# Step 7's transposes of queries and keys from TensorE to the DMA queue, with its attention one dense piece later

## The chip, the cores and the metric

The kernel runs on one core of one Trainium2 chip. The metric is the time of one execution on the device in microseconds (us), the median of three runs; lower is better. A separate execution was taken by the hardware profiler, and every line of a profile below comes from that one.

The core has TensorE (PE in the profile, its weight loads PEld), VectorE (DVE), ScalarE (ACT), GpSimd (POOL), SyncE (SP) and 16 DMA engines. Engines work through their own instruction streams in order and wait for each other by semaphores. SP issues nearly all DMAs of this kernel.

## What is computed

A decayed linear attention over 4 batches, 8 heads, 768 positions and 64 channels, and behind it a GELU layer without biases:

```python
for b in range(nb):                      # blocks of 64 positions
    intra = einsum('bhic,bhjc->bhij', qb, kb) * Dmask     # lam**(i-j), i >= j
    out[:, :, sl] = einsum('bhij,bhjd->bhid', intra, vb) \
                  + einsum('bhid,bhde->bhie', qb * lam_pow, kv_state)
    kv_state = lam_block * kv_state + einsum('bhsd,bhse->bhde', kb * rev_pow, vb)
x = out.transpose(0, 2, 1, 3).reshape(3072, 512)
h = x @ w_in                             # 512 -> 2048
g = gelu_tanh(h)
y = g @ w_out                            # 2048 -> 512
```

All inputs and the output are float32 in DRAM; the kernel casts to float16 for TensorE.

## The kernel before, in words

The attention is cut into 24 **steps**. A step is one batch, 256 positions and four of the eight heads; steps 2n and 2n+1 are the two halves of the heads of block n. For each step:

- `load_step` (L59, the DMA at L70) loads q, k and v of the step, 256 KB each, on SP's queue. Each of the three has four buffers (pool `ld`), so a load of step s waits until the cast of step s-4 has read its buffer.
- `cast_q` (L282, VectorE) scales q by the decay and casts it, `cast_k` (L295, mostly ScalarE) casts k, `scale_v` (L266, GpSimd) scales and casts v. `prep(s)` is all of them, with the transposing DMA between and further loads after it.
- q and k are needed with channels on partitions. Up to step 7, `stage_t` (L309) does this with eight TensorE transposes (L321) into PSUM and a copy back by ScalarE (L328, steps 5, 6) or VectorE (L330, steps 4, 7). From step `FIRST_DMA_T` = 8 on (L39), `transpose_dma` (L297) issues one DMA transpose on SP (L303) right behind the casts, and `stage_t` does nothing.
- `scores` (L344, matmuls L350) multiplies k by q for the step, `causal` masks the result (L360, VectorE), `products` (L365) multiplies by v, and `update` (L535) carries the state on (`t` on VectorE, `u` on GpSimd).

`R(n, s)` puts scores of step n, products of step n and the second products of step s = n-1 into the streams, then the masks and half of the state's update; `U(n)` is the other half. In later stages `burst` takes two steps at a time.

The GELU layer runs in seven groups of 256 or 512 tokens. `queue_group` cuts the group's matmuls into **dense pieces** (a list called `filler`), and `fill(n)` puts the next n pieces into TensorE's stream. A piece of the first product (`mm1`, L609, matmuls L613) in the groups of 256 tokens is eight matmuls into one PSUM bank, then a GELU on ScalarE (L617). A second product is eight matmuls (L692) of gT or of a sum of parts of gT that VectorE forms (L662): the product is done by a scheme with seven partial products in place of eight.

The order is written out by hand at the end of the kernel (L1043 on), and `pin` keeps it. The scheduler does not move anything. Around the change it reads: `prep(7)`, two pieces, `R(6, 5)`, `U(6)`, a piece, `prep(8)`, a piece, `stage_t(7)`, two pieces, `R(7, 6)` with `prep_qk(9)` between its scores and products, `store_pair(0)` (two output stores on SP), `U(7)`, `scale_v(9)`, two pieces, and then the loop over steps 8 to 12.

SP's queue, in order, around the change: loads of step 8; loads of step 9 (from `prep_v(6)`, L256); q and k of step 10 (from `prep_v(7)`); the DMA transpose of step 8; loads of step 11; the DMA transpose of step 9; v of step 10; the two output stores; the DMA transpose of step 10.

All PSUM tiles share one pool of eight banks (tag M), taken in turn.

Of the kernel before, what the change touches and what calls it, by code (L numbers as in the profile page):

```python
# [15 lines left out]
def kernel(  # L16
# [19 lines left out]
    NF = DFF // P  # L36
    NC = DM // P
    NSTEP = B * NSB * 2
    FIRST_DMA_T = 8  # L39
    PSUM = bass.MemoryType.PSUM  # L40

    const = ctx.enter_context(tc.tile_pool(name="const", bufs=1))
# [17 lines left out]
    def load_step(s, names="qkv"):  # L60
        b, r = divmod(s, 2 * NSB)
        sb, half = divmod(r, 2)
        ts = ld32.setdefault(s, [])
        for nm, src in (("q", q), ("k", k), ("v", v)):
            if nm not in names:
                continue
            t = ld.tile([P, HH, 2, D], FP32, tag=nm + "32", name=f"{nm}32_{s}")
            rows = src[b, half * HH : (half + 1) * HH, sb * SB : (sb + 1) * SB, :]
            queue = nc.scalar if (nm, s) == ("v", 0) else nc.sync
            pin(queue.dma_start(out=t[:].rearrange("p h j d -> p h (j d)"),  # L70
                                in_=rows.rearrange("h (p j) d -> p h (j d)", j=2)))
            ts.append(t)
# [49 lines left out]
    def sum_wout(j, m, eng):  # L122

        a, op, b = W_SUMS[m]
        r = slice(4 * j, 4 * j + 4)

        def rows(t):
            if t in w_slot:
                return w_sum16[:, w_slot[t], r, :]
            f, e = t  # L130
            return w_out16[:, f * HF + r.start : f * HF + r.stop, e * HE : e * HE + HE]

        pin(eng.tensor_tensor(rows(m), rows(a), rows(b), op))
# [36 lines left out]
    def load_ahead(s):  # L170
        if s < NSTEP:
            load_step(s)
# [72 lines left out]
    def prep(s):  # L245
        prep_qk(s)
        prep_v(s)
# [7 lines left out]

    def prep_v(s):  # L256
        scale_v(s)
        if s >= 6:
            if s + 3 == FIRST_DMA_T + 2:
                load_step(s + 3, "qk")  # L260
            else:
                load_ahead(s + 3)

    def scale_v(s):
        tv = a16p.tile([P, 2, HH, D], FP16, tag="v16", name=f"v16_{s}")
        pin(nc.gpsimd.tensor_tensor(wide(tv[:]), ld32[s][2][:], decay(dv, s), ALU.mult))  # L266
        a16[s] = a16[s] + (tv,)

    def prep_qk(s):
        cast_qk(s)  # L270
        transpose_dma(s)

    def cast_qk(s):
        cast_q(s)
        cast_k(s)
# [23 lines left out]
    def transpose_dma(s):  # L299
        tqk = whole_qk.pop(s)  # L300
        if s >= FIRST_DMA_T:
            o = qkp.tile([P, 2, 2, 2, P], FP16, tag="qkT", name=f"qkT_{s}")
            pin(nc.sync.dma_start_transpose(out=o[:].rearrange("p a j h t -> p (a j h) t"),  # L303
                                            in_=tqk[:].rearrange("p a j h d -> p (a j h d)")))
            qkT[s] = o
            if s == FIRST_DMA_T + 1:
                load_step(s + 1, "v")

    def stage_t(s):  # L309
        if s >= FIRST_DMA_T:  # L310
            return
        tq, tk = a16[s][:2]
        if s < 4:
            Tps = [ps_M.tile([P, 2, 2, P], FP16, tag="M", name=f"Tps{i}") for i in range(2)]
        else:
            Tps = ps_M.tile([P, 2, 2, 2, P], FP16, tag="M", name="Tps")
        for i, t in enumerate((tq, tk)):
            to = Tps[i] if s < 4 else Tps[:, i]
            for hp in range(2):
                for j in range(2):  # L320
                    pin(nc.tensor.transpose(to[:, j, hp, :], t[:, j, 2 * hp : 2 * hp + 2, :],  # L321
                                            ident[:]))
        o = qkp.tile([P, 2, 2, 2, P], FP16, tag="qkT", name=f"qkT_{s}")
        if s < 4:
            pin(nc.scalar.activation(out=o[:, 0], in_=Tps[0][:], func=AF.Copy))
            pin(nc.vector.tensor_copy(out=o[:, 1], in_=Tps[1][:]))
        elif s in (5, 6, 8):
            pin(nc.scalar.activation(out=o[:], in_=Tps[:], func=AF.Copy))  # L328
        else:
            pin(nc.vector.tensor_copy(out=o[:], in_=Tps[:]))  # L330
        qkT[s] = o
# [12 lines left out]
    def scores(n):  # L344
        o = qkT[n]
        Sps = [ps_M.tile([P, 2, 2, P], FP32, tag="M", name=f"S{hl}") for hl in range(2)]
        for hp in range(2):
            for jk in range(2):
                for hl, c in TILES:
                    pin(nc.tensor.matmul(  # L350
                        Sps[hl][half64(c), hp, jk, :], o[half64(hl), 1, jk, hp, half64(c)],
                        o[half64(hl), 0, :, hp, half64(c)], start=True, stop=True,
                        skip_group_check=True))
        Ss[n] = Sps

    def causal(n):

        t = ptp.tile([P, 2, 2, 2, P], FP16, tag="PT", name=f"PT_{n}")
        for hl, Sps in enumerate(Ss.pop(n)):
            pin(nc.vector.tensor_tensor(  # L360
                t[:, hl].rearrange("p b c d -> p b (c d)"), Sps[:].rearrange("p b c d -> p b (c d)"),
                mask[:].unsqueeze(1).to_broadcast([P, 2, 2 * P]), ALU.mult))
        PTs[n] = t
# [171 lines left out]
    def update(s, c, parts="tu"):  # L535


        sbg, half = divmod(s, 2)
        sb = sbg % NSB
        if c == 1 and sb == NSB - 1:  # L540
            Kps.pop(s)
            return
        if "t" in parts:
            K = (Kps[s] if c == 0 else Kps.pop(s))[c].rearrange("p (hp d) -> p hp d", hp=2)
            t = ucp.tile([P, 2, D], FP32, tag=f"t{half}", name=f"t_{s}_{c}")
            if sb == 0 and c == 0:
                pin(nc.vector.tensor_copy(out=t[:], in_=K))
            else:
                for hp in range(2):
                    pin(nc.vector.scalar_tensor_tensor(  # L550
                        t[:, hp, :], state[half][:, hp, :],
                        lamu[:, 2 * half + hp : 2 * half + hp + 1], K[:, hp, :],
                        ALU.mult, ALU.add))
            state[half] = t
        if "u" in parts:
            if (s if c == 0 else s + 2) in NARROW:
                u = ubp.tile([P, 2, 2, D], FP16, tag=f"u{half}", name=f"u_{s}_{c}")[:, 0]
                pin(nc.gpsimd.tensor_tensor(  # L558
                    u, state[half][:],
                    lamu[:, 2 * half : 2 * half + 2].unsqueeze(2).to_broadcast([P, 2, D]),  # L560
                    ALU.mult))
                us[(s, c)] = u
                return
            u = ubp.tile([P, 2, 2, D], FP16, tag=f"u{half}", name=f"u_{s}_{c}")
            pin(nc.gpsimd.tensor_tensor(  # L565
                u[:], state[half][:].unsqueeze(2).to_broadcast([P, 2, 2, D]),
                lumask[:, 2 * half : 2 * half + 2, :].unsqueeze(3).to_broadcast([P, 2, 2, D]),
                ALU.mult))
            us[(s, c)] = u
# [21 lines left out]
    def store_pair(pair):  # L591
        rows = out[2 * pair * P : 2 * pair * P + 2 * P, :].rearrange("(i p) d -> p i d", p=P)
        for i in range(2):
            pin(nc.sync.dma_start(out=rows[:, i], in_=o_pairs[pair][:, i]))
# [368 lines left out]
    def fill(n):  # L963
        for _ in range(min(n, len(filler))):
            filler.pop(0)()

    def R(n, s, ahead=None, keep=False):

        def first():
            if n is not None:  # L970
                scores(n)
            if ahead:
                ahead()

        if s in NARROW:
            products(n, s, between=first)
        else:
            first()
            products(n, s)
        if n is not None:  # L980
            causal(n)
        if s is not None and s % 2 == 1:
            g, i = group_of[s // 2]
            if i == len(groups[g]) - 1 and g > 0:
                queue_group(g)
        if n is not None and not keep:
            update(n, 0)

    def U(n):
        update(n, 1)  # L990


    idle(2, 512)
    prep(0)
    stage_t(0)
    chunk_decay()
    idle(1)
    prep(1)
    R(0, None)
    idle(0, 384)  # L1000
    stage_t(1)
    idle(3)
    U(0)
# [3 lines left out]
    causal(1)  # L1007
    idle(2)
    stage_t(2)
    prep_qk(3)  # L1010
    update(1, 0)
# [64 lines left out]
    fill(1)  # L1076
    prep(8)
    fill(1)
    stage_t(7)
    sum_wout(1, 4, DVE)  # L1080
    fill(2)
    R(7, 6, lambda: prep_qk(9))
    store_pair(0)
    U(7)
    scale_v(9)
    fill(2)

    FILL = {8: (2, 0, 0, 0), 9: (1, 2, 1, 2), 10: (0, 1, 1, 3), 11: (0, 1, 1, 3), 12: (0, 2, 1, 3)}
    for n, (a, b, c, d) in FILL.items():
# [135 lines left out]
```

## Time and profile before

| | |
|---|---|
| median of three runs | 198.35 us (198.2 to 198.77) |
| the profiled execution's own time | 198.35 us |
| its span, first to last instruction | 196.5 us |
| granted TensorE clock | 1.000 |
| TensorE transposes (L321) | 64, eight for each of steps 0 to 7 |
| DMA transposes (L303) | 16, steps 8 to 23 |

How to read the profile: the page shows the busy time of each engine, and the span in 40 slices of 4.9 us with the busy share of each engine in tenths. The timeline gives start, duration, engine, line, operation, tiles (written <- read) and count, with the idle time before it and what ended that in brackets; "SPq" rows are DMAs being issued by SP, and their time is that of the issue, not of the transfer. The DMA view adds the time from the issue to the landing of the last byte.

### The profile page before, as it was taken

What the parts mean: (1) busy time and instruction counts of PE and PEld (TensorE: products, weight loads), DVE (VectorE), ACT (ScalarE), POOL (GpSimd) and SP (SyncE); (2) the same over time, 40 slices, a digit from 0 to 9 for tenths busy, and PEclk for the clock granted to TensorE, in tenths of its full rate; (3) what the DMA queues carried; (4) which work ended last, traced back from release to release, by engine and by line L of the source; (5) the groups of instructions that cost most, each with busy time, mean ns of one, the idle gap of its engine ahead of it and who ended that gap; (6) DMA issues with size and microseconds to landing.
All of it is one profiled execution on the core that took longest, in us unless ns stands there. A gap on an engine that the chain in (4) does not pass through costs nothing.

```text
span 196.5 us, 5993 instructions
## 1 busy us (share of the span) xinstructions
PE 190.4 (97%) x2467; PEld 139.2 (71%) x2469; DVE 145.7 (74%) x291; ACT 125.7 (64%) x248; POOL 68.5 (35%) x85
## 2 busy tenths in 40 slices
PE   8979999999999999999999999999999999999993
PEld 2556544456888888754688754578888888888882
DVE  4897722888989879959989826999557996487620
ACT  3663878358774796676856379844877856679221
POOL 6594213457444832528523416064002030002000
PEclk9999999999999999999999999999999999999999
DMA  5999999999999999989999999900520300020205
GB/s 166 291 323 385 384 385 386 302 293 276 267 218 239 262 199 220 239 137 220 361 240 273 251 333 164 227 6 0 36 95 32 110 5 0 3 107 31 79 15 198
DMA packets 62810, 38.13 MB, mean 194 GB/s; under 512 B 18624, under 2 KB 55744, under 8 KB 62784
## 3 DMA queue, kind: packets, MB, share of 16 engines
q1 hardware_dynamic: 62240, 37.50, 76.1%
q8 instruction: 19, 0.31, 0.6%
q10 hardware_dynamic: 544, 0.26, 0.5%
q14 instruction: 7, 0.06, 0.1%
HBM read 27.26 MB, written 6.29 MB: 171 GB/s over the span
## 4 chain that ended last, share of the span: by engine, by line
PE 89%; SPq 4%; DMA 4%; ACT 0%; issue 0%
PE Hps L613 25%; PE MX L692 18%; PE MY L692 9%; PE HX L796 7%; PE O2ps L628 7%; PE MW L692 4%; DMA wi<-in_moe_w_in_dram 4%; SPq L70 4%; PE HY L796 4%; PE S L350 3%; PE Hps L895 3%; PE HW L796 2%; PE O L460 1%; PE OK L400 1%; PE Tps L321 1%; PE OK L422 1%
## 5 line engine op out<-in xcount | busy, mean ns | idle before, releaser
L613 PE MATMUL Hps<-xT,w_in 128*128 128x512 f16 (+1 forms) x288 | 50.5, 332 | 0.0
L613 PEld LDWEIGHTS <-w_in 128*128 128x128 f16 x288 | 27.8, 98 | 19.4
L617 ACT ACTIVATE gT<-Hps 128x512 f16<-128x512 f32 x56 | 32.6, 597 | 9.2 <-PE Hps L613 8.7
L360 DVE TENSOR_TENSOR PT<-S,mask 128x512 f16<-128x512 f32 x48 | 30.3, 681 | 8.8 <-PE S L350 8.8
L266 POOL TENSOR_TENSOR v<-v,dv 128x512 f16<-128x512 f32 x24 | 27.4, 1147 | 19.9 <-DMA v<-in_v_dram 11.5
L692 PEld LDWEIGHTS <-gs 128*128 128x128 f16 x320 | 31.1, 98 | 3.7
L692 PEld LDWEIGHTS <-gT 128*128 128x128 f16 x240 | 23.1, 98 | 3.5 <-ACT gT L617 0.2
L565 POOL TENSOR_TENSOR u<-t,lumask 128x256 f16<-128x256 f32 x21 | 15.6, 758 | 22.1 <-DVE t L550 13.0
L692 PE MATMUL MX<-w_sum,gs 128*128 128x256 f16 x160 | 21.4, 273 | 0.0
L295 ACT ACTIVATE qk<-k 128x512 f16<-128x512 f32 x23 | 14.4, 625 | 7.3 <-DMA k<-in_k_dram 7.1
L282 DVE TENSOR_TENSOR qk<-q,dq 128x512 f16<-128x512 f32 x23 | 17.9, 780 | 1.1 <-DMA q<-in_q_dram 1.1
L749 POOL TENSOR_TENSOR o<-u,q 128x512 f32<-128x512 f32 (+1 forms) x5 | 5.6, 1120 | 37.3 <-issue 34.8
L662 DVE TENSOR_TENSOR gs<-gT 128x1024 f16<-128x1024 f16 (+1 forms) x24 | 16.4, 689 | 3.0 <-ACT gT L617 3.0
L558 POOL TENSOR_TENSOR u<-t,lamu 128x128 f16<-128x128 f32 x19 | 11.2, 597 | 18.7 <-DVE t L550 8.9
L628 PE MATMUL O2ps<-w_out,gT 128*128 128x512 f16 x64 | 14.6, 379 | 0.0
L796 PEld LDWEIGHTS <-ws 128*128 128x128 f16 x128 | 12.4, 98 | 1.7 <-DVE xs L775 0.3
L529 ACT ACTIVATE xT<-OK 128x256 f16<-128x256 f32 x22 | 8.7, 454 | 6.4 <-PE OK L413 3.1
L714 ACT ACTIVATE u<-MX 128x256 f32<-128x256 f32 x18 | 6.9, 383 | 7.4 <-PE MX L692 7.4
L628 PEld LDWEIGHTS <-gT 128*128 128x128 f16 x64 | 6.1, 98 | 6.6
L692 PE MATMUL MY<-w_out,gs 128*128 128x256 f16 x80 | 10.7, 273 | 0.0
L810 DVE COPY u<-HX 128x512 f32<-128x512 f32 x8 | 5.5, 689 | 6.8 <-ACT gT L814 4.4
L350 PEld LDWEIGHTS <-qkT 64*64 64x64 f16 x384 | 6.3, 106 | 5.8 <-issue 2.8
(105 smaller groups left out, 328.5 us busy)
## 6 DMA issues: line engine op xcount, KB each, us to landing
q<-in_q_dram SPq DMA_DIRECT2D x24, 256.0 KB, 4.9
k<-in_k_dram SPq DMA_DIRECT2D x24, 256.0 KB, 5.1
v<-in_v_dram SPq DMA_DIRECT2D x23, 256.0 KB, 5.3
out_dram<-o SPq DMA_DIRECT2D x23, 256.0 KB, 4.5
wo<-in_moe_w_out_dram SPq DMA_DIRECT2D x4, 1024.0 KB, 9.5
wi<-in_moe_w_in_dram SPq DMA_DIRECT2D x4, 512.0 KB, 8.1
wi<-in_moe_w_in_dram SPq DMA_DIRECT2D x2, 1024.0 KB, 13.8
v<-in_v_dram ACTq DMA_DIRECT2D x1, 256.0 KB, 4.3
```

What stands on the lines that cost most here:

```text
L266: pin(nc.gpsimd.tensor_tensor(wide(tv[:]), ld32[s][2][:], decay(dv, s), ALU.mult))
L282: pin(q_eng.tensor_tensor(wide(tq), q32[:], decay(dq, s), ALU.mult))
L295: pin(nc.scalar.activation(out=wide(tk), in_=k32[:], func=AF.Copy))
L350: pin(nc.tensor.matmul(Sps[hl][half64(c), hp, jk, :], o[half64(hl), 1, jk, hp, half64(c)], o[half64(hl), 0, :, hp, half64(c)], start=True, ...
L360: pin(nc.vector.tensor_tensor(t[:, hl].rearrange("p b c d -> p b (c d)"), Sps[:].rearrange("p b c d -> p b (c d)"), mask[:].unsqueeze(1).t ...
L565: pin(nc.gpsimd.tensor_tensor(u[:], state[half][:].unsqueeze(2).to_broadcast([P, 2, 2, D]), lumask[:, 2 * half : 2 * half + 2, :].unsqueez ...
L613: pin(nc.tensor.matmul(by_block(Hps[:, i, :]), w_in16[:, c, f * P : (f + 1) * P], x(c), start=(c == 0), stop=(c == NC - 1)))
L617: pin(nc.scalar.activation(out=dst, in_=Hps[:], func=AF.Gelu_apprx_tanh))
L628: pin(nc.tensor.matmul(O2[tau][0][:], gT[:, f % HF, f // HF, tau * P : (tau + 1) * P], w_out16[:, f, :], start=(n == 0), stop=(n == NF - 1)))
L662: pin(nc.vector.tensor_tensor(g_rows(m, i), g_rows(a, i), g_rows(b, i), op))
L692: pin(nc.tensor.matmul(dst, lhsT, rhs, start=(opens and i == 0), stop=(closes and i == HF - 1), skip_group_check=True))
L796: pin(nc.tensor.matmul(dst[:, i, :], w_in_block(a, slice(c, c + 1), slice(f * P, f * P + P))[:, 0], x_block(b, slice(c, c + 1))[:, 0], sta ...
```

## The change

`FIRST_DMA_T` goes from 8 to 7: step 7 is transposed by the DMA, issued in `prep_qk(7)`, and its eight TensorE transposes and the copy of their result go. The loads of step 9, which `prep_v(6)` issued before, are issued right behind this transpose. One dense piece moves from behind `R(7, 6)` to ahead of it. `prep_qk(9)`, which stood between scores and products of `R(7, 6)`, is put behind `R(7, 6)`, `U(7)` and one piece. That v of step 10 is loaded behind the transpose of step 9 stays as it is.

```diff
-    FIRST_DMA_T = 8
+    FIRST_DMA_T = 7
...
     def prep_v(s):
         scale_v(s)
-        if s >= 6:
-            if s + 3 == FIRST_DMA_T + 2:
-                load_step(s + 3, "qk")
-            else:
-                load_ahead(s + 3)
+        if s == 7:
+            load_step(s + 3, "qk")
+        elif s > 7:
+            load_ahead(s + 3)
...
             qkT[s] = o
-            if s == FIRST_DMA_T + 1:
+            if s == 7:
+                load_step(s + 2)
+            elif s == 9:
                 load_step(s + 1, "v")
...
-        elif s in (5, 6, 8):
+        elif s in (5, 6):
...
     prep(8)
     fill(1)
-    stage_t(7)
     sum_wout(1, 4, DVE)
-    fill(2)
-    R(7, 6, lambda: prep_qk(9))
+    fill(3)
+    R(7, 6)
+    U(7)
+    fill(1)
+    prep_qk(9)
     store_pair(0)
-    U(7)
     scale_v(9)
-    fill(2)
```

## The prediction

> **What bounds the kernel now.** I read the page first: engine shares, then the slices.
>
> ```profile
> span 196.5 us, 5993 instructions
> ...
> PE 190.4 (97%) x2467; PEld 139.2 (71%) x2469; DVE 145.7 (74%) x291; ACT 125.7 (64%) x248; POOL 68.5 (35%) x85
> ...
> PE   8979999999999999999999999999999999999993
> ...
> DMA  5999999999999999989999999900520300020205
> ```
>
> The reader is to see two full rows. TensorE is at 9 from the fourth slice (15 us) to the last, at granted clock 1.00, so every microsecond taken from its queue there is a microsecond of the span, unless it then waits for something. The DMA row is full too, up to slice 26 (127 us): transfers up to there stand in one line, and one more in that line makes all behind it late. The list of waits agrees: the waits of TensorE's weight loads after 30 us sum to about 5 us, mostly "issue" gaps of 0.1 to 0.4 us where the shape of the matmuls changes, and none is for a DMA. So I looked next at the place of the change, in TensorE's timeline:
>
> ```profile
> 50.15 0.61 PE L321 MATMUL Tps<-ident,qk 128*128 128x128 f16 x8
> 50.59 1.91 PE L613 MATMUL Hps<-xT,w_in 128*128 128x256 f16 x16
> 52.43 0.42 PE L350 MATMUL S<-qkT 64*64 64x128 f16 x16
> ...
> 58.69 0.42 PE L350 MATMUL S<-qkT 64*64 64x128 f16 x16
> ```
>
> The transposes of step 7 (L321) hold TensorE from 50.15 to 50.59, scores of step 7 start at 52.43, of step 8 at 58.69. Then SP's queue, and ScalarE's cast of k of step 7:
>
> ```profile
> 45.02 0.78 SPq L70 DMA_DIRECT2D v<-in_v_dram  x1
> 45.89 0.71 SPq L70 DMA_DIRECT2D q<-in_q_dram  x1
> ...
> 49.22 0.58 SPq L70 DMA_DIRECT2D k<-in_k_dram  x1
> 50.81 1.76 SPq L303 DMA_TRANSPOSE qkT<-qk  x1
> 52.63 0.56 SPq L70 DMA_DIRECT2D q<-in_q_dram  x1
> ```
>
> ```profile
> 47.09 0.63 ACT L295 ACTIVATE qk<-k 128x512 f16<-128x512 f32 x1 [0.15 <-ACT qkT L328]
> ```
>
> Here v of step 8 is issued, then q of step 9, up to k of step 10; then the DMA transpose of step 8. Landings are the issue plus the "us to landing" that the DMA view gives for that one issue: v of step 8 at 45.02 + 5.0 = 50.0, k of step 10 at 49.22 + 5.1 = 54.3, transpose of step 8 at 50.81 + 4.5 = 55.3, q of step 11 at 52.63 + 4.8 = 57.5.
>
> **The change, part by part.**
>
> 1. *Eight transposes leave TensorE.* They cost it the distance to the next matmul, 50.59 - 50.15 = 0.44 us (not 8 times the row's mean of 219 ns, as they overlap). This is on the path: **-0.44 us**, and it is the most that the change can give.
> The Trainium skill, "TensorE: Matmul & The Clock Gate", Part 4 (PE-mode transpose), gives about 275 ns for one 128x128 transpose inside a kernel; by that the gain would be 8 x 0.275 = 2.2 us (an estimate from the page). The row of this case, 55 ns each in sequence, decides.
>
> 2. *VectorE's copy of them* (L330, 50.79, 0.69 us) goes as well. VectorE is not on the path there: worth 0.
>
> 3. *One dense piece (8 matmuls, 0.87 us) moves ahead of the attention.* It is moved, not added: 0. Scores of step 7 now start at 52.43 - 0.44 + 0.87 minus the wait for the old copy, about 52.8 (eight matmuls at 49.27, then 24 from 50.15 at 0.109 us). Five pieces instead of six stay between them and scores of step 8, which are wanted at 58.69 - 0.44 = 58.25.
>
> 4. *A new wait: scores of step 7 on a DMA.* The transpose can be issued when k of step 7 is cast, 47.09 + 0.63 = 47.7, plus 0.2 (step 8: cast ends 50.6, issue 50.8): 47.9. Its price from both sides:
>
> ```profile
> L303 SPq DMA_TRANSPOSE qkT<-qk x16: 1232/1622/3359, 50.8 to 139.2; - x16
> ...
> DMA to landing us min/median/max: 4.1/4.6/6.0
> ```
>
> so it lands between 52.0 and 53.9; needed at 52.8. The 4.1 belong to issues with at most 3 us of loads ahead of them (at 80.00 and 83.39), 5.6 and more to those with over 4 us ahead. At 47.9 only q, k, v of step 8 are in flight, the last landing at 50.0, that is 2.1 us: I take 4.1 to 4.5, **landing 52.0 to 52.4, no wait**, with 0.4 to 0.8 us to spare. At 6.0 it is a wait of 1.1 us, and all of TensorE stands behind it.
>
> 5. *The queue behind it.* The transpose passes q, k, v of step 9 and q, k of step 10 on SP, which issue at about 49.3 instead of 45.9. Before, these five came from 50.0 to 54.3, 0.86 each. Now they start from 52.0-52.4; the first load behind a transpose landed 0.9 us after it behind step 10's, 2.2 behind step 8's. So k of step 10 lands at 52.2 + 0.9 to 2.2 + 4 x 0.86 = 56.5 to 57.8, **late by 2.2 to 3.5 us**; I take 2.2 to 2.5, as the new transpose stands in a queue that has nearly drained. Transpose of step 8 follows 1.0 behind as before: 57.5 to 58.8, wanted at 58.25. I take 57.7: no wait; upper end 0.5.
> The page "DMA: Bandwidth & Descriptors" of the Trainium skill, section "Latency and other measured facts", gives DMA transposes an effective 261 GB/s. For these 256 KB that is 1.0 us (an estimate), with which nothing below would be late and the full 0.44 us would come; the 2.15 us between the landings at 55.3 and 57.5 say otherwise.
>
> What else has cover for 2.2 to 2.5 us? Landing against scores, before: step 9 60.1/64.3, step 10 64.7/68.7, step 11 68.8/74.1, step 12 73.9/80.0, step 14 84.1/87.3. The smallest spare is 3.2 us, 2.8 when TensorE is 0.44 earlier: enough. The exception is step 16:
>
> ```profile
> 87.82 1.57 SPq L303 DMA_TRANSPOSE qkT<-qk  x1
> ```
>
> ```profile
> 93.55 0.64 PE L350 MATMUL S<-qkT 64*64 64x128 f16 x32
> ```
>
> It landed at 87.82 + 5.8 = 93.6; these 32 matmuls are steps 15 and 16, so step 16 starts 0.2 after 93.55, at about 93.8. **Only 0.15 us to spare.** What the queue is late there, TensorE waits. But the queue stands still before it:
>
> ```profile
> 83.50:84.50 1.00, 1.00 (x6) 0.47 (x5) 1.00 (x2) 0.60 (x1) 1.00 (x2) 1.00 0.01 2
> ```
>
> (last columns: DMA share 0.01, 2 GB/s). The transpose of step 15 waits there for its own casts. And the loads issued at 71.66 and 78.32 landed in 3.2 and 3.5 us, against 5.0 in the full queue, so the line is short there too; I take half a microsecond from each. So 2.2 to 2.5 late shrinks by about 2, to 0.2 to 0.5 at step 16; the bounds are -0.44 (it comes earlier, with the casts that follow TensorE) and +1.5 (only the 1 us of standstill is won back). With 0.15 us of spare, being 0.2 to 0.5 late would leave TensorE no gain at all here; but a queue that stands still waits for casts, and these come 0.44 earlier. I take the middle between keeping all and losing two thirds: **0.15 us** of the 0.44.
>
> 6. *q and k casts of step 9 move behind the attention.* VectorE's (L282, 52.40, 0.68 us) now runs after masks and state of step 7, at about 55.3; its load lands at 53.1 to 54.4, so it does not wait, but the sums of gT behind it (L662) and the masks of step 8 (59.25) move by about 0.5. The tightest reader is the product that starts at 62.13 and wants, 0.44 later, the sum that ended at 61.73: 0.8 us to spare, minus 0.5, minus 0.44 of gain. Between 0 and 0.4 us; I take **0.1**. ScalarE's k cast has gT evictions behind it, 0.6 us of every 0.87, which catch up: 0.
>
> Sum: -0.44 + 0.15 + 0.1 = **-0.2 us**. The profiled execution took 198.35 us, the same as the median of the runs shown, so 198.35 - 0.2 = **198.15 us**.
>
> **The rivals.**
>
> - *The whole queue stays late up to step 16* (slower). For it: DMA share about 1 in nearly every slice before 83.5, and 0.15 us of spare. Against: the 1 us standstill. It decides from 0.15 us late at step 16, where the time goes above that of before; from part 5's bounds, 0.7 to 1.5 late gives +0.55 to +1.35: 198.9 to 199.7, middle 199.3.
> - *The new transpose is late itself*, 5.6 to 6.0 us: a wait of 0.7 to 1.1 at scores of step 7, and the load queue as much later, which gives 0 to 0.7 again at step 8: net +0.3 to +1.4, 199.1.
> - *The change gives nothing*: what TensorE wins is taken by VectorE's chain (part 6, upper end) and step 16: 198.35 to 198.7.
> - *More than 0.44*: only if the transposes cost TensorE more than their distance, or small gaps close: 197.4 to 197.7.
>
> **How the numbers follow.** 0.3% of this kernel is 0.6 us, about what a measurement of it can tell from no change. The forecast (197.9 to 198.5) gets 0.46, step 16 late 0.28, step 7 late 0.12, nothing gained 0.10, more than 0.44 0.04. Faster by over 0.3% means below 197.75: the last case and a bit of the first, 0.05. Slower means above 198.95: three quarters of the second and of the third case plus a tail of the fourth, 0.33. Within: 0.62. The range goes from 197.8 to 199.6: it leaves out the last case, the upper part of the step 16 case and the end of the step 7 case.
>
> **What would show it.** Right: no L321 after 46 us, matmuls of L613 without a gap from 49.3 to 52.8, scores of step 7 at 52.8 with the transpose landed by 52.4, scores of step 8 at 58.2 to 58.3, steps 15 and 16 without a gap between them near 93.3. Wrong: TensorE waiting for a DMA at L350 (as "PEld L350 <- DMA qkT") at step 7, 8 or 16, or for VectorE at a product near 62; the place tells which case it is. The DMA slices at 83.5 to 84.5 no longer empty would show part 5 right.

## The result, and the profile after

The changed kernel takes **201.22 us** (median of 6 runs, 200.44 to 202.16) against 198.51 us for the kernel before in the same session: a ratio of 1.0136, 95% interval 1.0104 to 1.0168. It is slower by about 2.7 us, where the prediction had 198.15. The profiled execution took 200.44 us with a span of 198.7 us, 2.1 and 2.2 us more than before; what follows explains these 2.2 us. It is the fastest of the six: the other five had spans of 199.1 to 200.4 us, and of those no trace was kept.

The page of the changed kernel: span, engines, and the slices of TensorE and of the DMA engines.

```profile
span 198.7 us, 5980 instructions
...
PE 189.7 (95%) x2459; PEld 138.2 (70%) x2461; DVE 144.4 (73%) x290; ACT 125.9 (63%) x248; POOL 69.3 (35%) x85
...
PE   8878999999979999999999999999999999999993
...
DMA  5999999999999999999999999820412200020205
```

TensorE is busy 0.7 us less and the span is longer. The slice that fell from 9 to 7 is the twelfth, 54.6 to 59.6 us, just behind the change. The DMA row reads 9 in every slice from the 2nd to the 25th, where before had one 8 among them (slice 18, around 85 us): the standstill there is gone.

The list of waits for TensorE's matmuls from 45 to 100 us (in total, times, longest), empty before, has two lines now:

```profile
PE S L351 <- DMA qkT<-qk: 1.6, 1, 1.6
PE MX L693 <- DVE gs L663: 0.6, 1, 0.6
```

TensorE's timeline shows the first (lines behind the change are one higher than before: L351 scores, L614 and L693 dense matmuls):

```profile
49.28 3.66 PE L614 MATMUL Hps<-xT,w_in 128*128 128x256 f16 x32
52.87 0.42 PE L351 MATMUL S<-qkT 64*64 64x128 f16 x16
...
57.18 1.13 PE L693 MATMUL MX<-w_out,gT 128*128 128x256 f16 x8
59.89 0.42 PE L351 MATMUL S<-qkT 64*64 64x128 f16 x16 [1.57 <-DMA qkT<-qk]
```

Up to the scores of step 7 (52.87) all is as forecast: the matmuls run without a gap, and no wait for the new transpose. The scores of step 8 would come at 59.89 - 1.57 = 58.32 and wait 1.57 us for their own. SP's queue there, and what the DMA engines do in 40 parts of the stretch from 55.2 to 58.8 us:

```profile
47.79 1.44 SPq L302 DMA_TRANSPOSE qkT<-qk  x1
49.29 0.56 SPq L70 DMA_DIRECT2D q<-in_q_dram  x1
...
51.58 0.51 SPq L70 DMA_DIRECT2D k<-in_k_dram  x1
52.25 3.38 SPq L302 DMA_TRANSPOSE qkT<-qk  x1
```

```profile
DMA  9999999993938226511401999900000001000000
...
q8 instruction: 1, 0.02, 4.0%
```

k of step 10, issued at 51.58, landed 5.9 us later at 57.45; the transpose of step 8 behind it landed at 59.84, 7.6 us after its issue. The engines are full up to 56.0 us, run empty by 57.0, come back for 0.4 us near 57.3 and stand idle again. In this stretch lies one packet of the queue "instruction": 16 KB of TensorE's program (the page counts 19 such packets, 0.31 MB), at 55.88, for 2.28 us on one of the 16 engines. The transpose is 1024 packets of 256 bytes. The first 512 ended by 57.2 us, and most of the rest ran at once. But 21 packets that began at 57.46 to 57.52 all ended only at 58.95 to 58.99, while some 25 ran one or two at a time from 58.1 on, when the fetch ended (58.15). I infer from it that these stood on the engine with the fetch, and that it held up all.

The second wait has a longer way. One line each of ScalarE's, VectorE's and TensorE's timeline:

```profile
75.62 0.63 ACT L294 ACTIVATE qk<-k 128x512 f16<-128x512 f32 x1 [0.77 <-DMA k<-in_k_dram]
```

```profile
76.77 1.11 DVE L663 TENSOR_TENSOR gs<-gT 128x512 f16<-128x512 f16 x1 [1.09 <-ACT gT L618]
```

```profile
79.85 0.61 PE L693 MATMUL MX<-w_sum,gs 128*128 128x256 f16 x4 [0.59 <-DVE gs L663]
```

k of step 13 landed at 75.46. ScalarE stood before its cast, the GELU behind it came late, VectorE's sum after that, and the product at 79.85 last. The list of waits gives 0.6 us on matmuls and 0.9 on weight loads. Scores of steps 7, 8, 11, 12 and 15 are 0.44, 1.20, 1.28, 2.18 and 2.19 us later than before: ahead of its wait step 8 stood 0.37 us earlier than before, and with the two waits, 1.57 and about 0.9, that is the whole difference; from step 12 on nothing is added.

### The profile page after: what moved, and what is told of

The parts are those of the page before. It is cut to its first block, busy times and chain, and to the rows that moved or that the text cites. A ratio compares the mean times of both kernels' runs of the same rounds, so it can differ in the third digit from the quotient of the medians.

```text
span 198.7 us, 5980 instructions
## 1 busy us (share of the span) xinstructions
PE 189.7 (95%) x2459; PEld 138.2 (70%) x2461; DVE 144.4 (73%) x290; ACT 125.9 (63%) x248; POOL 69.3 (35%) x85
## 4 chain that ended last, share of the span: by engine, by line
PE 84%; DMA 8%; SPq 4%; DVE 1%; issue 1%; ACT 0%; DVEq 0%
PE Hps L614 22%; PE MX L693 17%; PE MY L693 8%; PE HX L797 7%; PE O2ps L629 7%; PE MW L693 4%; DMA wi<-in_moe_w_in_dram 4%; SPq L70 4%; DMA qkT<-qk 4%; PE HY L797 4%; PE S L351 3%; PE Hps L896 3%; PE HW L797 2%; PE O L461 1%; PE OK L401 1%; PE OK L423 1%
## 5 line engine op out<-in xcount | busy, mean ns | idle before, releaser
L614 PE MATMUL Hps<-xT,w_in 128*128 128x512 f16 (+1 forms) x288 | 50.3, 332 | 0.0
L614 PEld LDWEIGHTS <-w_in 128*128 128x128 f16 x288 | 27.8, 98 | 19.4
L693 PEld LDWEIGHTS <-gs 128*128 128x128 f16 x320 | 31.1, 98 | 4.5 <-DVE gs L663 0.9
L693 PEld LDWEIGHTS <-gT 128*128 128x128 f16 x240 | 23.0, 98 | 3.7 <-ACT gT L618 0.5
L693 PE MATMUL MX<-w_sum,gs 128*128 128x256 f16 x160 | 21.6, 273 | 0.6 <-DVE gs L663 0.6
L750 POOL TENSOR_TENSOR o<-u,q 128x512 f32<-128x512 f32 (+1 forms) x5 | 6.4, 1283 | 37.4 <-issue 34.8
L281 DVE TENSOR_TENSOR qk<-q,dq 128x512 f16<-128x512 f32 x23 | 18.4, 802 | 1.2 <-DMA q<-in_q_dram 1.1
L351 PE MATMUL S<-qkT 64*64 64x128 f16 x384 | 9.1, 220 | 2.4 <-DMA qkT<-qk 1.6
L351 PEld LDWEIGHTS <-qkT 64*64 64x64 f16 x384 | 6.3, 106 | 7.3 <-issue 2.8
L693 PE MATMUL MY<-w_out,gs 128*128 128x256 f16 x80 | 10.7, 273 | 0.0
```

Source lines behind the costliest of these rows:

```text
L281: pin(q_eng.tensor_tensor(wide(tq), q32[:], decay(dq, s), ALU.mult))
L351: pin(nc.tensor.matmul(Sps[hl][half64(c), hp, jk, :], o[half64(hl), 1, jk, hp, half64(c)], o[half64(hl), 0, :, hp, half64(c)], start=True, ...
L614: pin(nc.tensor.matmul(by_block(Hps[:, i, :]), w_in16[:, c, f * P : (f + 1) * P], x(c), start=(c == 0), stop=(c == NC - 1)))
L693: pin(nc.tensor.matmul(dst, lhsT, rhs, start=(opens and i == 0), stop=(closes and i == HF - 1), skip_group_check=True))
```

## The experiments

Two theories. **LINE** (called QUEUE in experiments 1 to 3): the line of transfers is full from 45 to 80 us, one more transpose makes all behind it late, and the waits come where the spare is least. **FETCH**: the line has the room, but an instruction fetch that falls into a transpose makes it about 1.5 us longer, and that was the accident at step 8. Behind each expectation stand the median time and its ratio to the kernel before on the same chip, with the 95% interval.

**1. Moving the fetch with short matmuls at the start**, in the changed kernel (a) and in the one before (b). The wide warming matmul becomes 32 short ones of 64 columns (`idle_short`):

```diff
-    idle(2, 512)
+    idle_short(32)    
+    idle(2)
```

> The changed kernel, with one wide warming matmul at the very start replaced by 32 short ones, so that TensorE's stream has some 62 more instructions ahead of everything and its 16 KB instruction fetches (queue q8) come about 62 instructions earlier; the short matmuls compute nothing that is used. In the changed kernel's profile a fetch starts at 55.88 and takes 2.28 us, inside the DMA transpose of step 8, which landed 7.6 us after its issue. Theory FETCH (the transpose was late because the fetch held one of the 16 DMA engines in its middle): the fetch comes at 52 to 54, the transpose lands in 5 to 6 us, the wait at scores of step 8 falls from 1.6 to under 0.5 us, and the time to 199 to 200. Theory QUEUE (the line of loads behind the added transpose is late, whatever the fetch does): the wait stays at 1.2 to 2 us and the time at 200.5 to 201.5.

> The kernel before with the same 32 short matmuls at the start; they compute nothing that is used. Both theories: transposes have 3 us of room in it, so 198.1 to 198.8. If it is slower by over 0.6, where fetches fall matters to the kernel before as well, at step 16, which has only 0.15 us of room.

a: 199.93 us, 1.0030 [0.9987, 1.0074]; b: 200.37 us, 1.0070 [1.0035, 1.0105]. In the profiled execution of each the granted clock fell to 0.6 in the slice from 15 to 20 us, and step 7 began 2 us late, so the medians tell little. Six executions of a kept a mean clock of 0.997 or more; they took 198.18 to 199.97 us, all below the fastest of the changed kernel (200.44), and the three such of b 198.36 to 199.23. In the trace of a the transpose of step 8 landed 0.89 us behind its load, and the wait is 0.3 us. That fits FETCH, but as no trace of an undisturbed execution was kept, it does not decide.

**2. The order alone**: the kernel before, its TensorE transposes and loads kept, with step 7's attention one piece later and the casts of step 9 behind it.

```diff
-    fill(2)
-    R(7, 6, lambda: prep_qk(9))
-    store_pair(0)
+    fill(3)
+    R(7, 6)
     U(7)
+    fill(1)
+    prep_qk(9)
+    store_pair(0)
     scale_v(9)
-    fill(2)
```

> The kernel before with the order of the changed kernel alone: one dense piece ahead of the attention of step 7, casts of step 9 behind it; step 7 stays on TensorE and the loads stay where they were. QUEUE and FETCH: the order is not the cause, 198.2 to 198.7. Rival CASTS (VectorE's chain became the bound because the cast of q of step 9 moved behind the masks): 199 to 200.5.

199.05 us, 1.0025 [1.0007, 1.0043], in the range of CASTS. The order costs about half a microsecond, here, on TensorE:

```profile
62.15 1.34 PE L692 MATMUL MY<-w_out,gs 128*128 128x256 f16 x8
63.33 1.35 PE L692 MATMUL MX<-w_sum,gs 128*128 128x256 f16 x8
```

These two groups took 1.04 each in the kernel before: their weight loads wait 0.4 us twice for VectorE's sums, which stand behind the moved cast. From the scores of step 8 to those of step 9 it is 6.27 us instead of 5.65.

**3. Scores of step 8 later**: in the changed kernel two dense pieces move from behind that attention to ahead of it.

```diff
-        fill(b + (n == 8) - (n == 10))
+        fill(b + (n == 8) * 3 - (n == 10))
...
             scale_v(n + 2)
-            fill(2)
```

> The changed kernel with two dense pieces (1.74 us) that stood behind the attention of step 8 moved ahead of it, so scores of step 8 are wanted at 60.0 and the transpose landed at 59.8. If the wait at step 8 is the whole loss: it goes, 199.3 to 199.8. If the whole line of transfers is late (QUEUE, and FETCH too, as the fetch is not moved), the room that TensorE wins is lost again behind the load of k of step 13: the wait at step 8 goes, the wait for sums at 79 grows from 1.2 to 2 us or more, 200.3 to 201.2.

200.53 us, 1.0079 [1.0052, 1.0106]. No wait at step 8, but the list of waits shows it elsewhere:

```profile
PE OK L414 <- POOL u L559: 1.2, 1, 1.2
PE MX L693 <- DVE gs L663: 0.6, 1, 0.6
```

The wait for sums did not grow, as had been expected; the other line is new. It stands at 70.16, for GpSimd's part of the state's update:

```profile
69.27 0.84 POOL L559 TENSOR_TENSOR u<-t,lamu 128x128 f16<-128x128 f32 x1
```

GpSimd had worked without a gap since 65.77, when it began with a scaling of v whose load had landed at 65.61. So a wait taken away in one place returned at the next; that the load's landing set GpSimd's start is inferred from these two times.

**4. Step 8 on TensorE, step 7 by DMA**: as many DMA transposes as before. The same edit stands in `transpose_dma` and, with its `return`, in `stage_t`.

```diff
-        if s >= FIRST_DMA_T:
+        if s >= FIRST_DMA_T and s != 8:
```

> The changed kernel, but step 8 is transposed by TensorE (8 instructions, copied out by VectorE) and only step 7 goes from the TensorE side to the DMA queue: as many DMA transposes up to step 16 as in the kernel before, the order of the changed kernel. LINE theory (one more transpose of 2.2 to 2.4 us in a line of transfers that has little room from 45 to 80 us is the cause): no wait on DMA at the scores of step 8, k of step 13 lands at 71 to 73 us, no wait for sums around 79 us, and 198.2 to 199.4 us, 2 us below the changed kernel; the moved casts may keep 0.6 us of it. Rival PLACE (the place of step 7's transpose, ahead of the loads of step 9, or the moved attention is the cause): the loads of step 9 are as late as in the changed kernel and 200.3 us or more remain.

199.24 us, 1.0039 [1.0016, 1.0062]; no wait on a DMA, and 0.5 us of weight loads waiting for sums, as in experiment 2. The place of step 7's transpose ahead of the loads is not what costs.

**5. The transposes alone, in the order of before** (the diff of experiment 2 undone in the changed kernel).

> The changed kernel with the order of before around step 7: its transposes by DMA, ahead of the loads of step 9, but its attention after two dense pieces and the casts of step 9 ahead of it. LINE theory: step 7's scores are wanted at about 52.0 us and its transpose lands at about 51.8, so no wait or one of some tenths there; the transpose of step 8 stays at 6.5 to 7.6 us, its scores wait for it 1.0 to 1.6 us, sums are late near 79 us, and the time is 200.6 to 201.4 us as in the changed kernel. Rival ORDER (the moved casts and attention are most of the loss): 198.3 to 199.2 us.

199.93 us, 1.0073 [1.0039, 1.0106], between what LINE and ORDER had. The scores of step 7 start at 51.91 without a wait; TensorE's timeline then has

```profile
58.62 0.42 PE L351 MATMUL S<-qkT 64*64 64x128 f16 x16 [0.39 <-DMA qkT<-qk]
...
95.90 0.42 PE L351 MATMUL S<-qkT 64*64 64x128 f16 x16 [0.60 <-DMA qkT<-qk]
```

and between them 0.36 us for GpSimd at step 11 and 0.59 for sums near 79 us. So transposes and order share the loss: alone 1.7 and 0.6 us by their medians, together 2.7.

**6. The transpose of step 8 ahead of q and k of step 10** on SP, in the changed kernel.

```diff
-        if s == 7:
-            load_step(s + 3, "qk")
-        elif s > 7:
+        if s > 7:
             load_ahead(s + 3)
...
             if s == 7:
                 load_step(s + 2)
+            elif s == 8:
+                load_step(s + 2, "qk")
```

> The changed kernel, but the transpose of step 8 is issued ahead of the loads of q and k of step 10 instead of behind them (at about 51.1 us, its casts being done at 50.7, in place of 52.25). Two loads of 0.86 us each less ahead of it: it lands at 57.2 to 58.9 us, and the wait of 1.57 us at the scores of step 8 falls to 0 to 0.6. LINE theory (the transfers of the whole stretch set the end, not this one wait): k of step 10 lands 2 us later, a wait comes back by step 12, the scores of step 13 stay 1.5 us or more later than in the kernel before: 200.2 to 201.3 us. Rival LOCAL (the one transpose is behind too much, nothing else): 199.0 to 199.8 us.

199.37 us, 1.0064 [1.0038, 1.0091]. Step 8 does not wait any more (its scores start at 58.05), but VectorE's sums come late there too:

```profile
62.62 0.61 PE L693 MATMUL MY<-w_out,gs 128*128 128x256 f16 x4 [0.52 <-DVE gs L663]
```

with 0.23 us for GpSimd and 0.61 for sums more, up to 79 us. VectorE still works behind the moved casts of experiment 2, and it waits for one of the loads that were passed:

```profile
58.67 0.69 DVE L279 TENSOR_TENSOR qk<-q,dq 128x512 f16<-128x512 f32 x1 [0.30 <-DMA q<-in_q_dram]
```

The median lies in LOCAL's range, and the waits that came back are LINE's: scores of step 13 are 1.6 us behind the kernel before (88.63 against 87.03). Neither is refuted.

**7. An empty instruction** behind each output matmul of block 0, to move the fetch at no cost.

```diff
                 O2[tau][1] += 1
+                if g == 0:
+                    pin(nc.tensor.nop())
```

> The changed kernel with 64 empty TensorE instructions, one behind each output matmul of block 0's dense part (31 to 49 us), so that TensorE's instruction fetches come about a quarter of their distance, 2 us, earlier: the fetch at 55.9 us, inside the transpose of step 8, moves to about 54 us, ahead of it. If the empty instructions cost nothing themselves (the matmuls around them start 0.22 us apart; if not, the start of step 7's scores shows it), FETCH theory: the transpose of step 8 takes 6.2 to 6.8 us in place of 7.6, the wait at its scores is 0.2 to 0.7 us in place of 1.57, and the time is 199.5 to 200.4 us. LINE theory: the wait shrinks too, but the loads of step 13 are still 2 us or more behind the kernel before, the wait for sums near 79 us grows by what was won, and 200.6 to 201.4 us remain.

200.59 us, 1.0104 [1.0077, 1.0131]. The fetch did not go to 54 us; it stood at 57.05, still in the transpose, which still landed 2.4 us behind its load. A miss of the means: it tells nothing of the theories.

**8. The first two output stores later** (512 KB, from behind the casts of step 9 to behind the loads of step 13), in the changed kernel and, as a control, in the one before.

```diff
-    store_pair(0)
...
             load_step(n + 4, "qkv" if n < 10 else "qk")
+            if n == 9:
+                store_pair(0)
```

> The changed kernel, but the two stores of the first output pair (256 KB each, 0.65 us apart on landing) are issued behind the loads of step 13 instead of behind the casts of step 9: 1.3 us less in the line of transfers ahead of the loads of step 12 and 13. LINE theory: the scores of step 8 wait 1.5 us as before (the stores were behind that transpose), but k of step 13 lands at 74 us or sooner instead of 75.5, the wait for sums near 79 us (0.6 on matmuls, 0.9 on weight loads) falls to 0.2 or less, the scores of step 13 stand 1.2 to 1.5 us behind the kernel before instead of 2.2, and the time is 199.9 to 200.6 us. Rival CHAIN (the wait for sums comes from VectorE's own work behind the late attention of step 8, not from the transfers): the wait stays at 0.5 or more, 200.8 us or more.

> The kernel before with the same two stores issued behind the loads of step 13. Control: nothing on TensorE waits for a transfer in this stretch, so 198.0 to 198.6 us, the same as the kernel before. If transfers already cost the kernel before something here, it gains 0.3 us or more.

198.80 us, 1.0012 [0.9994, 1.0030], and 198.27 us, 0.9998 [0.9980, 1.0016] for the control. In the changed kernel the one line for a DMA in the list of waits is that of step 8:

```profile
PEld L351 <- DMA qkT<-qk: 1.1, 1, 1.1
```

The wait for sums is gone. Room in the line removes the second wait, as LINE says, and nearly all of the loss, more than it said. The wait at step 8 is 0.9 us on the matmuls here, where 1.5 was expected, though the stores stand behind that transpose.

**9. All three repairs together** (order of before, transpose of step 8 ahead of q and k of step 10, stores later), run twice, and the same without the repair at step 8.

> The changed kernel with three of its costs taken away: the order of before around step 7 (casts of step 9 ahead of its attention, attention after two dense pieces), the transpose of step 8 ahead of the loads of q and k of step 10, and the two stores of the first pair behind the loads of step 13. If the three waits found (transpose of step 8, casts behind attention, late loads of step 13) are the whole loss, 197.6 to 198.4 us, the 0.44 us of the eight transposes at best. If the line of transfers is full over the whole stretch, a wait comes back in another place and 198.8 to 199.6 us remain.

> The kernel with step 7's transposes by DMA, the order of before around step 7 and the two stores of the first pair behind the loads of step 13, but the transpose of step 8 left behind the loads of q and k of step 10, as in the changed kernel: the version with all three repairs less the one at step 8. If the room made by the stores is enough by itself (LINE), 198.0 to 198.5 us: the wait of 0.4 us at the scores of step 8, seen with the order of before alone, stays, since the stores came behind that transpose, and the waits behind it (0.36 at step 11, 0.59 for sums near 79 us, 0.60 at step 16) go. If the late transpose of step 8 is a cost of its own that spreads, a second wait remains and 198.7 us or more.

> The version with all three repairs once more, beside the one without the repair at step 8 and with more rounds: 197.8 to 198.3 us, 0.05 to 0.25% below the kernel before, as measured the first time (198.09, interval of the ratio 0.9962 to 0.9997). If that gain was chance of the runs, the interval covers 1.

198.09 us, 0.9980 [0.9962, 0.9997], and again 198.15 us, 0.9974 [0.9955, 0.9993]; without the repair at step 8 198.23 us, 0.9988 [0.9965, 1.0011], its profile, of the slowest of its 12 executions, with a wait of 0.9 us there and none behind it. With all three no matmul waits from 45 to 100 us, and the eight transposes come out as a gain:

```profile
51.92 0.42 PE L351 MATMUL S<-qkT 64*64 64x128 f16 x16
...
58.18 0.42 PE L351 MATMUL S<-qkT 64*64 64x128 f16 x16
```

Both are 0.51 us ahead of the kernel before; 0.07 of it was there at step 6 already (47.41 against 47.48), which leaves the forecast 0.44. From step 11 on 0.28 us of the lead is left. This is the one version whose interval lies below the kernel before, by 0.2 and 0.26%.

**10. Moving the fetch by splitting matmuls.** A 128x512 output matmul of block 0 becomes two of 256 columns, for 32 or for all 64 of them: 64 or 128 TensorE instructions more, ahead of the change (the second with `tau < 4`).

```diff
-                pin(nc.tensor.matmul(O2[tau][0][:], gT[:, f % HF, f // HF, tau * P : (tau + 1) * P],
-                                     w_out16[:, f, :], start=(n == 0), stop=(n == NF - 1)))
+                parts = 2 if g == 0 and tau < 2 else 1
+                w = DM // parts
+                for e in range(parts):
+                    pin(nc.tensor.matmul(O2[tau][0][:, e * w : e * w + w],
+                                         gT[:, f % HF, f // HF, tau * P : (tau + 1) * P],
+                                         w_out16[:, f, e * w : e * w + w], start=(n == 0 and e == 0),
+                                         stop=(n == NF - 1), skip_group_check=True))
```

> The changed kernel, but the first 32 output matmuls of block 0's dense part (31 to 40 us, 128x512) are made in two halves of 256 columns: 64 TensorE instructions more, the same arithmetic, and by the 0.109 us of a 128x256 matmul in sequence no time. TensorE's later instruction fetches should come 64 instructions, about 2 us, earlier: the one at 55.9 us, inside the transpose of step 8, moves to about 54 us. FETCH theory (the fetch holds one of the 16 DMA engines and the transpose waits for it): the transpose of step 8, issued at 52.2, lands at 58.3 to 59.0 instead of 59.84, the wait of 1.57 us at its scores falls to 0.1 to 0.8, and the time to 199.3 to 200.6 us. Without FETCH (the transpose is as long wherever the fetch is): it lands at 59.5 or later, the wait stays 1.3 us or more, 200.5 to 201.5 us.

> The same with all 64 output matmuls of block 0 split: 128 TensorE instructions more, the fetch moves by some 4 us to about 52 us, well ahead of the transpose of step 8 on the engines (55 to 59 us). FETCH theory: the transpose lands at 58.0 to 58.7, the wait is 0 to 0.5 us, time 199.0 to 200.4 us, with sums late near 79 us still (0.3 to 0.6). Without FETCH: as the changed kernel, wait 1.3 us or more, 200.5 to 201.5 us.

198.68 us, 1.0015 [0.9995, 1.0034], and 198.67 us, 1.0018 [1.0001, 1.0036]: 2.5 us less than the changed kernel, with the same transfers in the same order. That is below FETCH's own ranges too; the profiled executions differ by less, 1.6 and 2.1 us in the span. With all 64 split, the stretch from 55.4 to 59.0 us of the DMA engines has one short gap, and no packet of the queue "instruction" is listed for it:

```profile
DMA  9999999999999961199999999999999999999999
```

k of step 10 landed at 57.23 and the transpose at 58.11, 0.88 behind it, and

```profile
57.16 1.14 PE L698 MATMUL MX<-w_out,gT 128*128 128x256 f16 x8
58.23 0.42 PE L351 MATMUL S<-qkT 64*64 64x128 f16 x16
```

step 8 starts without a wait where the prediction wanted it. With 32 split the transpose also lands 0.88 behind its load, but that load is later (57.98, with the fetch at 53.43 now among the loads), and 0.64 us of wait stay. FETCH is right about the length of the transpose.

**11. The split in three other kernels**: the one before, the order of before with DMA transposes (experiment 5), and the three repairs (experiment 9).

> The kernel before with the 64 output matmuls of block 0 split (128 TensorE instructions more, the fetches some 4 us earlier). Control: nothing on TensorE waits for a transfer there, so 198.0 to 198.6 us, the same as the kernel before, if the split costs and gives nothing by itself. Rival: the fetches cost the kernel before something too, and it gains 0.4 us or more; then the gain on the changed kernel is not all that of the change's own wait.

> Step 7's transposes by DMA, the order of before around step 7, and the split that moves the fetches. FETCH theory: the transpose of step 8 lands 0.9 to 1.1 us behind the load ahead of it and no wait is left at step 8 or behind it; with the casts of step 9 where they were, the 0.44 us of the eight transposes come out: 197.7 to 198.2 us, scores of step 8 at 57.7 to 58.3 us after those of step 7 at 51.9. LINE theory (the line has no room for one more transpose, wherever the fetches stand): a wait of 0.4 us or more returns by step 16, as without the split (0.36, 0.59 and 0.60): 198.6 us or more.

> The version with all three repairs (order of before, transpose of step 8 ahead of the loads of q and k of step 10, stores later) and the split. It had no wait left on TensorE for a transfer, so the split should give nothing: 197.8 to 198.3 us, as without it. If the three repairs and the split each take away something of their own, 197.4 us or less.

199.03 us, 1.0040 [1.0010, 1.0070]; 199.98 us, 1.0069 [1.0040, 1.0097]; 198.94 us, 1.0017 [0.9991, 1.0044]. The control shows that the split itself gives nothing and may cost 0.4% (its profile lost granted clock from 15 to 20 us, and step 7 began 0.6 us late). The second contradicts what FETCH forecast for its time, and its trace says why: the fetch moved out of the transpose of step 8 into that of step 7.

```profile
53.12 0.42 PE L351 MATMUL S<-qkT 64*64 64x128 f16 x16 [0.77 <-DMA qkT<-qk]
```

The fetch stands at 50.58, and the transpose landed 5.3 us after its issue, at 53.08. Behind it TensorE waits for no transfer up to the scores of step 15, and 0.3 us at step 16; LINE had forecast more. The span of this execution, 197.4 us, is 0.9 over that of before and its time of 199.89 us is 1.5 over; what lies outside the span no trace shows. The spans of all its executions have a median of 198.1 us, so this trace shows less than the usual loss. The third also missed its forecast: its interval covers 1, the gain of experiment 9 is not seen, and its trace has waits of 0.46 us for the transpose of step 7 and 0.2 each for a GELU and for sums.

**What the traces say together.** In the traces of both kernels and of all experiments I took each transpose issued from 45 to 100 us that stood in line behind a load or store (issued 3 us or more before that one landed) with both landings on record, and how far it landed behind that one. Where no 16 KB fetch of TensorE's program was under way at that time (from 0.2 us before the first landing to 0.6 after), 82 of 85 landed 0.70 to 1.17 us behind; where one was, 15 of 23 landed 2.29 to 2.58 us behind and 8 0.71 to 1.09. The three left of the 85 had fetches nearby too: at 1.91 and 1.95 an 8 KB fetch on another queue (14), and at 3.72 TensorE's, which began 0.69 us after the first landing. In the 8 short ones the transfer behind paid: where the next landing is on record, it came 2.03 to 2.82 us behind the transpose (0.33 to 1.02 behind the 15 long ones), and else the second one 2.46 to 3.08 behind.

Nor is it a matter of transposes alone. Loads and stores behind a load or a store, taken in the same way, landed 1.5 us or more behind in 33 of 53 cases with a fetch, and in 4 of 215 without. Where a fetch costs the line something, it is mostly about 1.5 us, and the transfer that it falls into, or the next, pays.

So neither theory alone. The change used up the room in the line (the k loads of steps 10 and 13 late); a fetch in the transpose of step 8 then took 1.4 us more than had been counted on. Taking away either brings back most of the loss: half a megabyte of stores moved out of the stretch, or the fetch moved to where there is room (with all 64 split it fell into the transpose of step 7, which landed at 52.39 for scores at 52.85).

## Why the prediction was wrong, point by point

- **Part 1 (0.44 us of transposes), 2 and 3: right.** With the order of before the scores of step 7 came 0.52 us earlier (experiment 5), of which 0.08 were there at step 6 already; with the order of the change at 52.87 as given, and step 8, where no fetch disturbed it, at 58.23 against 58.25. (The 219 ns called the row's mean are its median.)
- **Part 4 (no wait at step 7): right** in the changed kernel: issued at 47.79, no wait. The upper end of 6.0 us was no idle bound: 5.3 us and a wait of 0.77 with a fetch in it.
- **Part 5, k of step 10 late by 2.2 to 3.5 us: right**, 57.45 against 54.3, that is 3.1; but it is more than the 2.2 to 2.5 that I went on with, and this alone would have used up the room at step 8 (57.45 + 1.0 against 58.3).
- **Part 5, "Transpose of step 8 follows 1.0 behind as before", upper end 0.5: the step that failed.** It followed 2.39 behind, for a wait of 1.57. The 1.0 was a transpose not held up, and the longer landings in the range of issue to landing (up to 6.0) were put down to the loads ahead only. The profile of before had the sign: its transpose of step 8 landed 1.01 behind its load, but the next load 2.15 behind that, with a fetch at 54.61; I read these 2.15 us as an ordinary price of a transpose.
- **"What else has cover... enough": failed.** It held landings against scores, for the transposes only. The second wait came from a load, k of step 13, through ScalarE's cast, a GELU and VectorE's sum, to a product: about 0.9 us. The 3.2 us of spare at the transposes said nothing of that chain. Experiment 8 shows the cause: with the two stores out of the way this wait is gone.
- **Step 16 (0.15 us lost): did not come.** Its transpose landed at 94.97, its scores started at 95.98, since TensorE was late itself. The step was a weak place all the same: 0.60 us in experiment 5. The sign was right: DMA engines, empty before from 83.5 to 84.5 us, are busy in the changed kernel (share and GB/s last; a packet counts whole in the stretch in which it starts, so a share can pass 1).

```profile
83.50:84.50 1.00, 1.00 (x9) 0.68 (x7) 0.87 (x4) 0.78 (x4) 0.23 (x1) 1.00 1.21 289
```

- **Part 6 (0.1 us, at most 0.4): too small.** The moved casts cost 0.62 us in the trace of experiment 2 since the sum that ended at 61.73 ended at 62.83 there, 1.1 us later and not 0.5; and about 0.3 with the fetch moved (5.97 us from step 8 to step 9 against 5.65). In the changed kernel itself the distance is 5.65: VectorE caught up while TensorE waited at step 8.
- **The rivals.** "The whole queue stays late" had the kind (late transfers) and not the place (step 8 and a product between steps 11 and 12, not 16), and at 199.3 less than was lost. "The new transpose is late itself" did not happen in the changed kernel; it did in experiment 11, by a fetch.
- **The page on DMA transposes** ("DMA: Bandwidth & Descriptors" of the Trainium skill, "Latency and other measured facts"), by which 256 KB take an estimated 1.0 us, agrees with the undisturbed landings, 0.7 to 1.17 us behind the load; I had set it aside for the 2.15, which had a fetch beside it.

Not settled: the 0.6 us by which the median of the changed kernel lies further from before than its profiled execution, which no trace shows; and why 20 of the 53 loads and stores with a fetch beside them were not late.

## What to carry to other kernels

When a transfer is added to a line without gaps, follow every item behind it to its reader, loads and casts as well as the transposes, through the engines between; the wait comes where that chain has least spare, not where the change was made. A landing distance from one execution holds only with what shared the engines in it: look for instruction fetches in the stretch, and take both lengths as the range. And before moving work off a busy engine to a full queue, find something in that queue that can be later; here moving two output stores brought the changed kernel from 201.2 to 198.8 us.

## What the hardware showed that was not expected

- An instruction fetch of 16 KB takes one DMA engine 0.9 to 2.3 us, about every 8 us in this stretch, and the 256 KB transfer that it falls into, transpose or load, or the one behind, mostly lands about 1.5 us later. The Trainium skill, "Runtime: NRT & Kernel Launch", section "Instruction fetch mechanics", has fetches of 16 KiB for 256 instructions on a DMA queue of the sequencer's own, their cost mostly hidden. The size agrees, and the list of waits names none of TensorE for its own program here; what is not hidden is the delay of the transfers beside it.
- 64 and 128 more TensorE instructions (32 and 64 matmuls, each with its weight load) moved the fetch by 2.5 and 6 us to the front (55.88 to 53.43 and 49.72); 64 empty ones did not move it forward at all (57.05).
- With 32 short warming matmuls in place of a wide one the granted clock fell to 0.6 in the slice from 15 to 20 us of both profiled executions, and all behind began 2 us late; 11 of the 20 executions of the two kernels had a mean clock of 0.991 or less, against 2 of 31 of the kernel before.
